# Hash attention and MoE on one core: projections of two groups of pairs in three parts, transposes spread out, values prepared per pair

## The chip, the core and the metric

The kernel runs on one core of one Trainium2 chip; the other cores are idle and the granted TensorE clock (1.0 is full speed) is 0.998 to 1.0 in every run told here. The metric is device time in microseconds; a time is the median of several executions. All runs below are in the fast state. A time is 1.7 to 1.9 us longer than the span of the same execution's profile.

## The reference

Four batches of eight heads, 768 tokens, head size 64. Queries and keys are hashed to six bits by the sign of a projection, and a query sees only keys of its own bucket. The result goes through an MoE layer with a SiLU.

```python
q_bits = (np.einsum('bhsd,dk->bhsk', q, proj) > 0)          # 6 bits, likewise k
mask = q_bucket[:, :, :, None] == k_bucket[:, :, None, :]
scores = np.where(mask, scale * q @ k.T, -1e9)
attn = softmax(scores) @ v                                   # x = attn, heads side by side
h = x @ w_in                                                 # 3072 x 512 @ 512 x 2048
out = (h * sigmoid(h)) @ w_out
```

## The kernel before

Heads are taken in 16 pairs. A pair's q and k are transposed to `qk32` (64 rows of each head over one another), projected to bits, and the bits are written as extra rows beside q and k, so that one matmul gives score plus mask. The main loop counts units: each does one piece of 512 score columns, one exp on ScalarE (ACT) and four attention-times-value matmuls; nine units make a head. `plan(w, f)` puts preparation work ahead of unit `w`. In the traces here the instructions of an engine stand in the program's order (DVE's copies of unit 12's transposes, which TensorE started at 16.27 us, come only at 19.47, behind pair 1's bits), so the unit also decides the place in every engine's queue. From pair 6 on, q and k are transposed in blocks on DVE instead. The parts that matter:

```python
def warm_up(n):                       # ahead of any data, to open TensorE's clock
    for _ in range(n):
        nc.tensor.matmul(wps, warm, warm[:, None, :].to_broadcast([P, 4, P]), ...)
warm_up(5)
...
def t_unit(p, i):                     # 4 of the 12 transposes of a pair
    tp = ps.tile([P, 512], F32, tag="m", name="tp_ps", bufs=3)   # PSUM: three banks "m"
    for j in range(4): nc.tensor.transpose(tp[...], src[...], ident)
    nc.vector.tensor_copy(out=qk32[p][:, 512 * i : 512 * (i + 1)], in_=tp)
...
def v_unit(p, heads=(0, 1)):          # GpSimd, per head: cast v, and sum it over 6 blocks
    for i in heads:
        nc.gpsimd.tensor_copy(out=vv[:, :, 0:D], in_=src)
        nc.gpsimd.tensor_tensor(out=sa, in0=src[:, 0:3], in1=src[:, 3:6], op=ALU.add)
        nc.gpsimd.tensor_tensor(out=sb, in0=sa[:, 0], in1=sa[:, 1], op=ALU.add)
        nc.gpsimd.tensor_tensor(out=vs[:, i, 0:D], in0=sb, in1=sa[:, 2], op=ALU.add)
...
def proj_unit(*pairs):                # two pairs: 32 output rows for each of 4 (pair, q or k)
    for c0, w in ((0, 512), (512, S - 512)):
        bp = ps.tile([P, 512], F32, tag="m", name="bp_ps", bufs=3)
        ...                           # four narrow matmuls
    for bp, c0, w in bps:
        nc.vector.tensor_scalar(out=bt[...], in0=bp[...], ..., op0=ALU.is_gt, op1=ALU.subtract)
...
def av(w):
    if w % NU == 0:                   # first matmul of a head: needs vs, the sums of its v
        nc.tensor.matmul(o_ps[h][:, 0:NJ, :], dmat, vs[:, None, :].to_broadcast(...), ...)
...
for i in range(2):
    plan(8, lambda i=i: cast_unit(1, i))
    plan(8, lambda i=i: v_unit(1, (i,)))
plan(10, lambda: proj_halves(1))
for i in range(2):
    plan(11 + i, lambda i=i: bits_halves(1, i))       # each 4 instructions on VectorE (DVE)
for i in range(6):                                    # pairs 2, 3: units 12, 15, ..., 27
    plan(12 + 3 * i, lambda i=i: t_unit(2 + i // 3, i % 3))
    ...                                               # casts with the third of each pair
plan(28, lambda: proj_unit(2, 3))
...                                                   # pairs 4, 5: units 33, 36, ..., 48; projection in 60
```

The softmax here doesn't subtract the row's maximum and nothing guards it: scores larger than these inputs give would overflow.

Of the kernel before, what the change touches and what calls it, by code (L numbers as in the profile page):

```python
# [9 lines left out]
F32 = mybir.dt.float32  # L10
# [3 lines left out]
ALU = mybir.AluOpType  # L14
# [3 lines left out]
def kernel(  # L18
# [104 lines left out]
    def warm_up(n):  # L123
        for _ in range(n):
            nc.tensor.matmul(wps, warm, warm[:, None, :].to_broadcast([P, 4, P]),
                             start=True, stop=True)

    warm_up(5)
    ident = cst.tile([P, P], F32, name="ident")
    make_identity(nc, ident)  # L130

# [17 lines left out]
    NSL = 4  # L149
    QKA = [cst.tile([P, 2 * S], F16, name=f"qka{i}") for i in range(NSL)]  # L150
    QKB = [cst.tile([P, 2 * S], F16, name=f"qkb{i}") for i in range(NSL)]
    NVS = 8
    VV = [cst.tile([P, NJ, E1], F16, name=f"vv{i}") for i in range(NVS)]
    VS = [cst.tile([P, 2, E1], F16, name=f"vs{i}") for i in range(NVS // 2)]
    for i in range(NVS):
        nc.vector.memset(VV[i][:, :, D:E1], 1.0)
        nc.vector.memset(VS[i // 2][:, i % 2, D:E1], float(NJ))
    for i in range(NSL):
        (nc.vector if i < 2 else nc.gpsimd).memset(QKB[i][0:64, :], 0.0)
    ident16 = cst.tile([P, P], F16, name="ident16")  # L160
# [17 lines left out]
    def t_unit(p, i):  # L178
        if i == 0:
            qk32[p] = t32.tile([P, 2 * S], F32, tag="qk32", name="qk32")  # L180
        tp = ps.tile([P, 512], F32, tag="m", name="tp_ps", bufs=3)
        for j in range(4):
            n, t = divmod(4 * i + j, NJ)
            src = qk_sb[p, "qk"[n]]
            nc.tensor.transpose(tp[:, j * P : (j + 1) * P],  # L185
                                src[:, t].rearrange("p h d -> p (h d)"), ident)
        nc.vector.tensor_copy(out=qk32[p][:, 512 * i : 512 * (i + 1)], in_=tp)
# [64 lines left out]
                                scalar1=CS, scalar2=1.0,  # L252
                                op0=ALU.mult, op1=ALU.mult)

    def v_unit(p, heads=(0, 1)):
        for i in heads:
            h = 2 * p + i
            vv, vs = VV[h % NVS], VS[p % (NVS // 2)]
            src = v_sb[p][:, i, :].rearrange("p (t d) -> p t d", d=D)
            nc.gpsimd.tensor_copy(out=vv[:, :, 0:D], in_=src)  # L260
            sa = nrm.tile([P, 3, D], F32, tag="vsa", name="vsa")
            nc.gpsimd.tensor_tensor(out=sa, in0=src[:, 0:3], in1=src[:, 3:6], op=ALU.add)  # L262
            sb = nrm.tile([P, D], F32, tag="vsb", name="vsb")
            nc.gpsimd.tensor_tensor(out=sb, in0=sa[:, 0], in1=sa[:, 1], op=ALU.add)
            nc.gpsimd.tensor_tensor(out=vs[:, i, 0:D], in0=sb, in1=sa[:, 2], op=ALU.add)

    bits = {}
    CB = 256

    def proj_unit(*pairs):  # L270



        bt = btp.tile([P, 3, CB + 2], F16, tag="bits", name="bits")
        bps = []
        for c0, w in ((0, 512), (512, S - 512)):
            bp = ps.tile([P, 512], F32, tag="m", name="bp_ps", bufs=3)
            for i, p in enumerate(pairs):
                for n in range(2):
                    c = 32 * (2 * i + n)  # L280
                    nc.tensor.matmul(bp[c : c + 32, 0:w], pw[:, 0:32],  # L281
                                     qk32[p][:, n * S + c0 : n * S + c0 + w],
                                     start=True, stop=True)
            bps.append((bp, c0, w))
        r = slice(0, 64 * len(pairs))
        for bp, c0, w in bps:
            nc.vector.tensor_scalar(out=bt[r, c0 // CB : (c0 + w) // CB, 0:CB],
                                    in0=bp[r, 0:w].rearrange("d (x c) -> d x c", c=CB),
                                    scalar1=sc[r, 0:1], scalar2=sc[r, 1:2],
                                    op0=ALU.is_gt, op1=ALU.subtract)  # L290
        bits[pairs] = bt

    def proj_halves(p):

# [84 lines left out]

    def av(w):  # L380
        h, pts = parts(w)
        vv, vs = VV[h % NVS], VS[h // 2 % (NVS // 2)][:, h % 2, :]
        if w % NU == 0:
            o_ps[h] = ps.tile([P, NJ + 1, E1], F32, tag="o", name="o_ps", bufs=2)



            if direct(h):
                nc.tensor.matmul(o_ps[h][:, 0:NJ, :], dmat,  # L389
                                 vs[:, None, :].to_broadcast([P, NJ, E1]),  # L390
                                 start=True, stop=True)
        if w % NU == 4 and not direct(h):
            nc.tensor.matmul(o_ps[h][:, NJ, :], dmat, vs,
                             start=False, stop=True, skip_group_check=True)
        u = ut.pop(w)
        for jt, c0, n, o0 in pts:
            for i in range(n // P):
                nc.tensor.matmul(o_ps[h][:, c0 // P + i, :],  # L398
                                 u[:, o0 + i * P : o0 + (i + 1) * P], vv[:, jt, :],
                                 start=(not direct(h) and w % NU == 0 and i == 0), stop=True,  # L400
                                 skip_group_check=True)
        if w % NU == NU - 1:
            o = o_ps.pop(h)
            p, par = divmod(h, 2)
            if par == 0:
                x_pr[p] = xpl.tile([P, NJ, P], F16, tag="xpr", name="x_pr", bufs=4)
            if not direct(h):

                osum = nrm.tile([P, NJ, E1], F32, tag="osum", name="osum")
                vsum = nrm.tile([P, 1, E1], F32, tag="vsum", name="vsum")  # L410
                nc.vector.tensor_copy(out=vsum, in_=o[:, NJ : NJ + 1, :])
                nc.vector.tensor_tensor(  # L412
                    out=osum, in0=o[:, 0:NJ, :], in1=vsum.to_broadcast([P, NJ, E1]),
                    op=ALU.add)
                o = osum
            rec = nrm.tile([P, NJ], F32, tag="rec", name="rec")
            nc.vector.reciprocal(out=rec, in_=o[:, 0:NJ, D])  # L417
            (nc.vector if direct(h) else nc.gpsimd).tensor_tensor(  # L418
                out=x_pr[p][:, :, par * D : (par + 1) * D], in0=o[:, 0:NJ, 0:D],
                in1=rec[:, :, None].to_broadcast([P, NJ, D]), op=ALU.mult)  # L420
# [124 lines left out]
    t_first(0, 1, nc.vector.tensor_copy)  # L545
    warm_up(2)
    bt = proj_first(0)
    v_unit(0, (0,))
    for e in range(2):
        for n in range(2):  # L550
            cast_first(0, n, e, nc.scalar)
# [10 lines left out]
    def second_head():  # L562
        bt = proj_first(1)
        for e in range(2):
            for n in range(2):
                cast_first(1, n, e, nc.gpsimd)
                bits_first(bt, 1, n, e, nc.vector.tensor_copy)
        v_unit(0, (1,))

    at = {}  # L570

    def plan(w, fn):
        at.setdefault(w, []).append(fn)
# [4 lines left out]
        plan(4 + 2 * i, lambda i=i: t_unit(1, i))  # L578
    for i in range(2):
        plan(8, lambda i=i: cast_unit(1, i))  # L580
        plan(8, lambda i=i: v_unit(1, (i,)))
    plan(10, lambda: proj_halves(1))
    for i in range(2):
        plan(11 + i, lambda i=i: bits_halves(1, i))
        plan(0, lambda p=2 + i: load_qk(p))
        plan(3 + i, lambda p=2 + i: load_v(p))

    for i in range(6):
        plan(12 + 3 * i, lambda i=i: t_unit(2 + i // 3, i % 3))
        if i % 3 == 2:  # L590
            for par in range(2):
                plan(12 + 3 * i, lambda p=2 + i // 3, par=par: cast_unit(p, par))
    plan(28, lambda: proj_unit(2, 3))
    for i in range(4):
        plan(29 + i, lambda i=i: bits_unit((2, 3), i // 2, i % 2))
    for i in range(2):
        for j in range(2):
            plan(18 + 9 * i + 2 * j, lambda p=2 + i, j=j: v_unit(p, (j,)))
        plan(21 + i, lambda p=4 + i: load_qk(p))
    for i in range(4):  # L600
        plan((24, 40, 68, 74)[i], lambda i=i: load_w_in(i))
        plan(80 + 4 * i, lambda i=i: load_w_out(i))

    for i in range(6):
        plan(QST - 3 + 3 * i, lambda i=i: t_unit(4 + i // 3, i % 3))
        if i % 3 == 2:
            for par in range(2):
                plan(QST - 3 + 3 * i, lambda p=4 + i // 3, par=par: cast_unit(p, par))
    for Q in range(2, NQUAD):
        w0 = (Q - 1) * QST  # L610
        for i in range(4 if Q > 2 else 0):
            w1 = w0 + (5, 9, 12, 15)[i]
            plan(w1, lambda Q=Q, i=i: block_unit(2 * Q + i // 2, i % 2))
            if i % 2:
                for par in range(2):
                    plan(w1, lambda p=2 * Q + i // 2, par=par: cast_unit(p, par))
        wp = w0 + {2: 24, 3: 21}.get(Q, 20)
        plan(wp, lambda Q=Q: proj_unit(2 * Q, 2 * Q + 1))
        for i in range(4):
            plan(wp + {2: i, 3: 2 * i}.get(Q, 0),  # L620
                 lambda Q=Q, i=i: bits_unit((2 * Q, 2 * Q + 1), i // 2, i % 2))
        for i in range(2):
            plan(w0 + 5 + i, lambda p=2 * Q + i: load_v(p))
            for j in range(2):
                plan(w0 + 18 + 9 * i + 2 * j, lambda p=2 * Q + i, j=j: v_unit(p, (j,)))
            if Q + 1 < NQUAD:
                plan(w0 + (28 if Q == 3 else 8) + i, lambda p=2 * Q + 2 + i: load_blocks(p))
    for p in range(NPAIR):
# [73 lines left out]
```

## Time and profile before

| | before |
|---|---|
| time | 303.56 us (three runs, 303.19 to 303.80) |
| span of the profiled execution | 301.3 us |
| busy: TensorE (PE), DVE, ACT, GpSimd (POOL) | 98%, 60%, 70%, 43% |
| first exp | 8.26 us |
| first transposes of pair 4 (unit 33) | 28.88 us |
| first block transpose on DVE (unit 77) | 52.35 us |
| fourth block transpose on DVE (pair 7's k) | 61.82 us |

The lower four rows are landmarks that I use for every run: their differences cut the span into stretches, and a change in a stretch names the place where time went. The busy shares average over stages with different limits; the prediction reads the stages from the strips and the chain.

### The profile page before, as it was taken

What the parts mean: (1) busy time and instruction counts of PE and PEld (TensorE: products, weight loads), DVE (VectorE), ACT (ScalarE), POOL (GpSimd) and SP (SyncE); (2) the same over time, 40 slices, a digit from 0 to 9 for tenths busy, and PEclk for the clock granted to TensorE, in tenths of its full rate; (3) what the DMA queues carried; (4) which work ended last, traced back from release to release, by engine and by line L of the source; (5) the groups of instructions that cost most, each with busy time, mean ns of one, the idle gap of its engine ahead of it and who ended that gap; (6) DMA issues with size and microseconds to landing.
All of it is one profiled execution on the core that took longest, in us unless ns stands there. A gap on an engine that the chain in (4) does not pass through costs nothing.

```text
span 301.3 us, 7181 instructions
## 1 busy us (share of the span) xinstructions
PE 296.6 (98%) x2710; PEld 175.1 (58%) x2710; DVE 180.1 (60%) x344; ACT 210.1 (70%) x392; POOL 128.3 (43%) x203
## 2 busy tenths in 40 slices
PE   8999999999999999999999999999999999999996
PEld 3676855545665665555565665555566654446653
DVE  5797938899588355854694434954443443664332
ACT  5987989989886777778876666978977722452200
POOL 7589999388418551935158401755111100000000
PEclk9999999999999999999999999999999999999999
DMA  7999997999988638834078135011022003001112
GB/s 202 243 237 199 181 153 115 199 212 173 150 187 145 107 102 211 126 84 133 3 139 133 49 74 189 2 42 31 2 61 63 20 21 93 35 2 70 37 68 71
DMA packets 103170, 32.87 MB, mean 109 GB/s; under 512 B 90656, under 2 KB 100192, under 8 KB 103136
## 3 DMA queue, kind: packets, MB, share of 16 engines
q1 hardware_dynamic: 98752, 28.22, 44.6%
q0 software_dynamic: 4224, 4.19, 9.0%
q8 instruction: 21, 0.34, 0.5%
q14 instruction: 13, 0.11, 0.1%
q10 hardware_dynamic: 160, 0.00, 0.0%
HBM read 27.27 MB, written 6.29 MB: 111 GB/s over the span
## 4 chain that ended last, share of the span: by engine, by line
PE 88%; DVE 7%; DMA 1%; ACT 1%; issue 1%; SPq 1%; DVEq 0%; ACTq 0%
PE o_ps L496 26%; PE h_ps L461 24%; PE s_ps L366 19%; PE o_ps L398 12%; DVE g L470 3%; PE bp_ps L281 3%; PE tp_ps L185 2%; DMA k_row<-in_k_dram 1%; PE o_ps L482 1%; DVE qk L246 1%; DVE qka L343 1%; ACT u L369 1%; DVE osum L412 1%; SPq L79 0%; PE o_ps L389 0%
## 5 line engine op out<-in xcount | busy, mean ns | idle before, releaser
L369 ACT ACTIVATE u<-s_ps 128x512 f16<-128x512 f32 x288 | 157.0, 606 | 38.7 <-PE s_ps L366 38.3
L470 DVE SCALAR_TENSOR_TENSOR g<-th,h_ps 128x512 f16<-128x512 f32 x96 | 65.5, 687 | 73.8 <-ACT th L468 73.8
L461 PE MATMUL h_ps<-xT,win 128*128 128x512 f16 (+1 forms) x512 | 98.4, 325 | 0.1
L398 PEld LDWEIGHTS <-u 128*128 128x128 f16 x1152 | 68.1, 98 | 42.2 <-ACT u L369 8.4
L496 PE MATMUL o_ps<-wout,g 128*128 128x512 f16 x368 | 91.6, 379 | 0.0
L398 PE MATMUL o_ps<-vv,u 128*128 128x65 f16 x1152 | 82.6, 194 | 0.5 <-ACT u L369 0.4
L468 ACT ACTIVATE th<-h_ps 128x512 f32<-128x512 f32 x96 | 57.9, 603 | 35.9 <-PE h_ps L461 33.2
L461 PEld LDWEIGHTS <-win 128*128 128x128 f16 x512 | 49.9, 98 | 30.5 <-issue 0.4
L418 POOL TENSOR_TENSOR x_pr<-osum,rec 128x384 f16<-128x384 f32 x23 | 19.0, 826 | 88.5 <-DVE rec L417 88.0
L496 PEld LDWEIGHTS <-g 128*128 128x128 f16 x368 | 35.8, 98 | 33.7
L366 PE MATMUL s_ps<-qka 71*128 71x512 f16 x192 | 52.7, 327 | 0.0
L366 PE MATMUL s_ps<-qkb 128*128 128x512 f16 x192 | 52.6, 326 | 0.0
L251 POOL TENSOR_SCALAR qka<-qk 64x1536 f16<-64x1536 f32 x15 | 22.0, 1466 | 11.5 <-DVE qk L246 5.7
L501 DVE TENSOR_SCALAR osb<-o_ps 128x512 f32<-128x512 f32 x23 | 15.9, 691 | 15.0 <-PE o_ps L496 15.0
L251 POOL TENSOR_SCALAR qkb<-qk 64x1536 f16<-64x1536 f32 x15 | 22.1, 1471 | 1.2
L262 POOL TENSOR_TENSOR vsa<-v_sb 128x192 f32<-128x192 f32 x32 | 18.9, 591 | 0.0
L260 POOL CAST vv<-v_sb 128x384 f16<-128x384 f32 x32 | 16.2, 507 | 1.0 <-DMA v_sb<-in_v_dram 0.6
L246 DVE STREAM_TRANSPOSE qk<-k_blk 128x768 f32<-128x768 f32 x10 | 15.8, 1582 | 0.3 <-issue 0.3
L246 DVE STREAM_TRANSPOSE qk<-q_blk 128x768 f32<-128x768 f32 x10 | 16.0, 1596 | 0.0
L366 PEld LDWEIGHTS <-qka 71*128 71x128 f16 x192 | 15.5, 97 | 0.4 <-ACT qka L238 0.3
L366 PEld LDWEIGHTS <-qkb 128*128 128x128 f16 x192 | 15.4, 97 | 0.0
L412 DVE TENSOR_TENSOR osum<-o_ps,vsum 128x390 f32<-128x390 f32 x23 | 13.0, 565 | 2.3
(70 smaller groups left out, 162.5 us busy)
## 6 DMA issues: line engine op xcount, KB each, us to landing
out_dram<-osb SPq DMA_DIRECT2D x23, 256.0 KB
v_sb<-in_v_dram SPq DMA_DIRECT2D x15, 384.0 KB
q_blk<-in_q_dram SPq DMA_DIRECT2D x40, 96.0 KB
k_blk<-in_k_dram SPq DMA_DIRECT2D x40, 96.0 KB
win<-in_moe_w_in_dram POOLq DMA_DIRECT2D x4, 512.0 KB, 7.7
wout<-in_moe_w_out_dram POOLq DMA_DIRECT2D x4, 512.0 KB, 6.2
q_sb<-in_q_dram SPq DMA_DIRECT2D x5, 384.0 KB
k_sb<-in_k_dram SPq DMA_DIRECT2D x5, 384.0 KB
```

Of the source, the lines that this page charges most:

```text
L246: nc.vector.transpose(out=dst, in_=qk_sb[p, "qk"[n]])
L251: nc.gpsimd.tensor_scalar(out=dst[rows, :], in0=qk32[p][rows, :], scalar1=CS, scalar2=1.0, op0=ALU.mult, op1=ALU.mult)
L260: nc.gpsimd.tensor_copy(out=vv[:, :, 0:D], in_=src)
L262: nc.gpsimd.tensor_tensor(out=sa, in0=src[:, 0:3], in1=src[:, 3:6], op=ALU.add)
L366: nc.tensor.matmul(sp[:, o0 : o0 + n], t[rows, S + jt * P : S + (jt + 1) * P], t[rows, c0 : c0 + n], start=True, stop=True)
L369: nc.scalar.activation(out=u, in_=sp, func=AF.Exp, scale=ESC)
L398: nc.tensor.matmul(o_ps[h][:, c0 // P + i, :], u[:, o0 + i * P : o0 + (i + 1) * P], vv[:, jt, :], start=(not direct(h) and w % NU == 0 and ...
L418: (nc.vector if direct(h) else nc.gpsimd).tensor_tensor(out=x_pr[p][:, :, par * D : (par + 1) * D], in0=o[:, 0:NJ, 0:D], in1=rec[:, :, Non ...
L461: nc.tensor.matmul(hp[:, j, :], w_in16[:, dt, ft * P : (ft + 1) * P], xT[4 * b + dt][:, c0 : c0 + n], start=(dt == 0), stop=(dt == NDT - 1))
L468: nc.scalar.activation(out=th, in_=hp, func=AF.Tanh, scale=0.5)
L470: after.append(lambda: nc.vector.scalar_tensor_tensor(out=g[ci][:, grp * f : (grp + 1) * f, :], in0=th, scalar=1.0, in1=hp, op0=ALU.add, o ...
L496: nc.tensor.matmul(o2[tt], g[ci][:, ft, ct * P : (ct + 1) * P], w_out16[:, ft, :], start=(ft == 0), stop=(ft == NFT - 1))
```

## The change

The intent is to take the two long pauses out of ACT's stream of exps: each projection of two pairs becomes three parts of 256 columns some units apart, and the transposes that feed them alternate between the two pairs. The value preparation is done for both heads of a pair by instructions twice as large. The warm-up of TensorE partly uses narrow matmuls of 32 and 64 rows.

```diff
-    warm_up(5)
+    warm_up(1)
+    warm_rows(32, 2)     # 8 matmuls of 32 rows x 256 columns, in four row groups and PSUM banks
+    warm_up(1)
+    warm_rows(64, 2)     # 4 of 64 rows
+    warm_up(1)
...
-    def v_unit(p, heads=(0, 1)):
-        for i in heads:
-            ...
+    def v_unit(p, heads=slice(0, 2)):     # the same four instructions, for both heads at once
...
-    def proj_unit(*pairs):
+    def proj_unit(*pairs, parts=((0, 2), (2, 3))):
...
         plan(8, lambda i=i: cast_unit(1, i))
-        plan(8, lambda i=i: v_unit(1, (i,)))
+    plan(8, lambda: v_unit(1))
...
-    for i in range(6):
-        plan(12 + 3 * i, lambda i=i: t_unit(2 + i // 3, i % 3))
-        ...
-    plan(28, lambda: proj_unit(2, 3))
+    def prepare(p, steps, parts):
+        for k, w in enumerate(steps):
+            i, j = divmod(k, 2)
+            plan(w, lambda q=p + j, i=i: t_unit(q, i))
+            ...                           # casts with the third of each pair
+        for x, w in enumerate(parts):
+            plan(w, lambda x=x: proj_unit(p, p + 1, parts=((x, x + 1),)))
+    prepare(2, (12, 14, 16, 18, 21, 23), (20, 25, 28))
...
-    for i in range(6):
-        plan(QST - 3 + 3 * i, lambda i=i: t_unit(4 + i // 3, i % 3))      # 33 ... 48
-        ...
+    prepare(4, (33, 36, 39, 42, 48, 51), (45, 54, 58))    # and no projection in unit 60
...
-            for j in range(2):
-                plan(w0 + 18 + 9 * i + 2 * j, lambda ...: v_unit(p, (j,)))
+            plan(w0 + 18 + 9 * i, lambda p=2 * Q + i: v_unit(p))
```

More of the change, by code (lines that the diff above doesn't have):

```diff
@@ L126, in warm_up, with warm_rows @@
                              start=True, stop=True)
-    warm_up(5)
+    def warm_rows(size, n):
+        banks = [ps.tile([P, 2, P], F32, tag="s", name="warm_s", bufs=3) for _ in range(3)]
+        banks.append(wps[:, 0:2, :])
+        for _ in range(n):
+            for r in range(P // size):
+                w = warm[size * r : size * (r + 1)]
+                nc.tensor.matmul(banks[r], w, w[:, None, :].to_broadcast([size, 2, P]),
+                                 start=True, stop=True)
+    warm_up(1)
[3 more added lines that the diff above has]
+    warm_up(1)
     ident = cst.tile([P, P], F32, name="ident")
@@ L151 @@
     QKB = [cst.tile([P, 2 * S], F16, name=f"qkb{i}") for i in range(NSL)]
-    NVS = 8
-    VV = [cst.tile([P, NJ, E1], F16, name=f"vv{i}") for i in range(NVS)]
-    VS = [cst.tile([P, 2, E1], F16, name=f"vs{i}") for i in range(NVS // 2)]
+    NVS = 4
+    VV = [cst.tile([P, 2, NJ, E1], F16, name=f"vv{i}") for i in range(NVS)]
+    VS = [cst.tile([P, 2, E1], F16, name=f"vs{i}") for i in range(NVS)]
     for i in range(NVS):
-        nc.vector.memset(VV[i][:, :, D:E1], 1.0)
-        nc.vector.memset(VS[i // 2][:, i % 2, D:E1], float(NJ))
+        nc.vector.memset(VV[i][:, :, :, D:E1], 1.0)
+        nc.vector.memset(VS[i][:, :, D:E1], float(NJ))
     for i in range(NSL):
@@ L253, in cast_unit @@
                                 op0=ALU.mult, op1=ALU.mult)
-    def v_unit(p, heads=(0, 1)):
-        for i in heads:
-            h = 2 * p + i
-            vv, vs = VV[h % NVS], VS[p % (NVS // 2)]
-            src = v_sb[p][:, i, :].rearrange("p (t d) -> p t d", d=D)
-            nc.gpsimd.tensor_copy(out=vv[:, :, 0:D], in_=src)
-            sa = nrm.tile([P, 3, D], F32, tag="vsa", name="vsa")
-            nc.gpsimd.tensor_tensor(out=sa, in0=src[:, 0:3], in1=src[:, 3:6], op=ALU.add)
-            sb = nrm.tile([P, D], F32, tag="vsb", name="vsb")
-            nc.gpsimd.tensor_tensor(out=sb, in0=sa[:, 0], in1=sa[:, 1], op=ALU.add)
-            nc.gpsimd.tensor_tensor(out=vs[:, i, 0:D], in0=sb, in1=sa[:, 2], op=ALU.add)
+    def v_unit(p, heads=slice(0, 2)):
+        n = heads.stop - heads.start
+        vv, vs = VV[p % NVS][:, heads], VS[p % NVS][:, heads]
+        src = v_sb[p][:, heads].rearrange("p h (t d) -> p h t d", d=D)
+        nc.gpsimd.tensor_copy(out=vv[:, :, :, 0:D], in_=src)
+        sa = nrm.tile([P, n, 3, D], F32, tag="vsa", name="vsa")
+        nc.gpsimd.tensor_tensor(out=sa, in0=src[:, :, 0:3], in1=src[:, :, 3:6], op=ALU.add)
+        sb = nrm.tile([P, n, D], F32, tag="vsb", name="vsb")
+        nc.gpsimd.tensor_tensor(out=sb, in0=sa[:, :, 0], in1=sa[:, :, 1], op=ALU.add)
+        nc.gpsimd.tensor_tensor(out=vs[:, :, 0:D], in0=sb, in1=sa[:, :, 2], op=ALU.add)
     bits = {}
     CB = 256
-    def proj_unit(*pairs):
-        bt = btp.tile([P, 3, CB + 2], F16, tag="bits", name="bits")
+    def proj_unit(*pairs, parts=((0, 2), (2, 3))):
+        if pairs not in bits:
+            bits[pairs] = btp.tile([P, 3, CB + 2], F16, tag="bits", name="bits")
+        bt = bits[pairs]
         bps = []
-        for c0, w in ((0, 512), (512, S - 512)):
+        for x0, x1 in parts:
+            c0, w = x0 * CB, (x1 - x0) * CB
             bp = ps.tile([P, 512], F32, tag="m", name="bp_ps", bufs=3)
@@ L283, in proj_unit @@
                                      start=True, stop=True)
-            bps.append((bp, c0, w))
+            bps.append((bp, x0, x1))
         r = slice(0, 64 * len(pairs))
-        for bp, c0, w in bps:
-            nc.vector.tensor_scalar(out=bt[r, c0 // CB : (c0 + w) // CB, 0:CB],
-                                    in0=bp[r, 0:w].rearrange("d (x c) -> d x c", c=CB),
+        for bp, x0, x1 in bps:
+            nc.vector.tensor_scalar(out=bt[r, x0:x1, 0:CB],
+                                    in0=bp[r, 0 : (x1 - x0) * CB]
+                                    .rearrange("d (x c) -> d x c", c=CB),
                                     scalar1=sc[r, 0:1], scalar2=sc[r, 1:2],
                                     op0=ALU.is_gt, op1=ALU.subtract)
-        bits[pairs] = bt
     def proj_halves(p):
@@ L381, in av @@
         h, pts = parts(w)
-        vv, vs = VV[h % NVS], VS[h // 2 % (NVS // 2)][:, h % 2, :]
+        vv, vs = VV[h // 2 % NVS][:, h % 2], VS[h // 2 % NVS][:, h % 2, :]
         if w % NU == 0:
@@ L547 @@
     bt = proj_first(0)
-    v_unit(0, (0,))
+    v_unit(0, slice(0, 1))
     for e in range(2):
@@ L567, in second_head @@
                 bits_first(bt, 1, n, e, nc.vector.tensor_copy)
-        v_unit(0, (1,))
+        v_unit(0, slice(1, 2))
     at = {}
@@ L586 @@
         plan(3 + i, lambda p=2 + i: load_v(p))
-    for i in range(6):
-        plan(12 + 3 * i, lambda i=i: t_unit(2 + i // 3, i % 3))
-        if i % 3 == 2:
-            for par in range(2):
-                plan(12 + 3 * i, lambda p=2 + i // 3, par=par: cast_unit(p, par))
-    plan(28, lambda: proj_unit(2, 3))
+    def prepare(p, steps, parts):
+        for k, w in enumerate(steps):
+            i, j = divmod(k, 2)
+            plan(w, lambda q=p + j, i=i: t_unit(q, i))
+            if i == 2:
+                for par in range(2):
+                    plan(w, lambda q=p + j, par=par: cast_unit(q, par))
+        for x, w in enumerate(parts):
+            plan(w, lambda x=x: proj_unit(p, p + 1, parts=((x, x + 1),)))
+    prepare(2, (12, 14, 16, 18, 21, 23), (20, 25, 28))
     for i in range(4):
@@ L596 @@
     for i in range(2):
-        for j in range(2):
-            plan(18 + 9 * i + 2 * j, lambda p=2 + i, j=j: v_unit(p, (j,)))
+        plan(18 + 9 * i, lambda p=2 + i: v_unit(p))
         plan(21 + i, lambda p=4 + i: load_qk(p))
@@ L602 @@
         plan(80 + 4 * i, lambda i=i: load_w_out(i))
-    for i in range(6):
-        plan(QST - 3 + 3 * i, lambda i=i: t_unit(4 + i // 3, i % 3))
-        if i % 3 == 2:
-            for par in range(2):
-                plan(QST - 3 + 3 * i, lambda p=4 + i // 3, par=par: cast_unit(p, par))
+    prepare(4, (33, 36, 39, 42, 48, 51), (45, 54, 58))
     for Q in range(2, NQUAD):
@@ L617 @@
         wp = w0 + {2: 24, 3: 21}.get(Q, 20)
-        plan(wp, lambda Q=Q: proj_unit(2 * Q, 2 * Q + 1))
+        if Q > 2:
+            plan(wp, lambda Q=Q: proj_unit(2 * Q, 2 * Q + 1))
         for i in range(4):
@@ L623 @@
             plan(w0 + 5 + i, lambda p=2 * Q + i: load_v(p))
-            for j in range(2):
-                plan(w0 + 18 + 9 * i + 2 * j, lambda p=2 * Q + i, j=j: v_unit(p, (j,)))
+            plan(w0 + 18 + 9 * i, lambda p=2 * Q + i: v_unit(p))
             if Q + 1 < NQUAD:
```

## The prediction

> **What bounds the kernel now.** I read the page first.
>
> ```profile
> PE 296.6 (98%) x2710; PEld 175.1 (58%) x2710; DVE 180.1 (60%) x344; ACT 210.1 (70%) x392; POOL 128.3 (43%) x203
> DVE  5797938899588355854694434954443443664332
> ACT  5987989989886777778876666978977722452200
> ```
>
> TensorE looks full everywhere, but a matmul's modelled span hides waits behind it, so the 98% alone names no bound. The strips show stages: ACT is nearly full in slices 3 to 8 (15 to 60 us), DVE in slice 9 (60 to 68 us), neither later. The chain that ended last agrees: from 76 us on it is TensorE matmuls with 0.2 us steps of other engines between them, from 55 to 76 us it runs over DVE (g, block transposes, bits), before that over TensorE and ACT. The change edits the program before unit 72 (about 51 us) and the GpSimd work of all pairs. What it gains or loses must arise before 51 us and is then handed on by the later stages, whose work is unchanged.
>
> A unit is one score, one exp and one attention-times-value step. Third view: the timeline of ACT from 16 to 48 us. Columns: start, length, instruction, count, idle time just before.
>
> ```profile
> 16.19 9.54 ACT L369 ACTIVATE u<-s_ps 128x512 f16<-128x512 f32 x18 [0.64 <-PE s_ps L366]
> 27.39 16.27 ACT L369 ACTIVATE u<-s_ps 128x512 f16<-128x512 f32 x32 [1.65 <-PE s_ps L366]
> 44.76 3.54 ACT L369 ACTIVATE u<-s_ps 128x512 f16<-128x512 f32 x7 [1.11 <-PE s_ps L366]
> ```
>
> Two idle stretches, 1.65 and 1.11 us, each for a late score. Fourth view: the chain in order of time at the same two places (start, length, what).
>
> ```profile
> 24.83 0.22 PE s_ps L366
> 25.04 1.80 PE bp_ps L281 x15
> 26.84 0.23 PE o_ps L398 x4
> 27.07 0.23 PE s_ps L366 x2
> ...
> 42.58 0.22 PE s_ps L366
> 42.80 1.43 PE bp_ps L281 x16
> 44.22 0.23 PE o_ps L398 x4
> 44.45 0.21 PE s_ps L366
> ```
>
> So the projections of pairs 2,3 (unit 28) and 4,5 (unit 60) hold TensorE while ACT runs dry. 1.65+1.11 = 2.76 us is the most that spreading them can give. Fifth view: the timeline of DVE while pairs 2 and 3 are transposed.
>
> ```profile
> 16.52 1.46 DVE L320 COPY qka<-bits 13x384 f16<-13x384 f16 x4
> 18.01 0.34 DVE L320 COPY qkb<-bits 13x384 f16<-13x384 f16 x1
> 18.37 0.40 DVE L317 TENSOR_SCALAR qkb<-bits,sc 13x384 f16<-13x384 f16 x1
> 18.78 0.34 DVE L320 COPY qkb<-bits 13x384 f16<-13x384 f16 x1
> 19.14 0.41 DVE L317 TENSOR_SCALAR qkb<-bits,sc 13x384 f16<-13x384 f16 x1
> 19.47 1.27 DVE L187 COPY qk<-tp_ps 128x512 f32<-128x512 f32 x2
> 20.67 0.17 DVE L417 RECIPROCAL rec<-o_ps 128x6 f32<-128x6 f32 x1
> 20.87 0.56 DVE L418 TENSOR_TENSOR x_pr<-o_ps,rec 128x384 f16<-128x384 f32 x1
> 21.35 1.28 DVE L187 COPY qk<-tp_ps 128x512 f32<-128x512 f32 x2
> ```
>
> DVE is late here. TensorE did the first transposes (unit 12) at 16.27, DVE copied them out only at 19.47, after the bits of pair 1. This backlog decides my number.
>
> **What the Trainium skill says.** "TensorEngine Tiling (Array Packing)", Key Properties: changing the tiling mode drains TensorE. The trace agrees in size: score to score over the projection at 42.58 takes 1.87 us, a bare unit 0.34 (17.33 to 17.67), so the projection costs 1.53. At full clock its columns need 12 waves of 256 column times; at the 0.43 us that one 512-column wave pair shows between its weight loads (42.73, 43.18, 43.61) that is 1.28. The remaining 0.25 is entering and leaving the narrow mode. "TensorE: Matmul & The Clock Gate", Part 3, The mechanism: a weight load overlaps running matmuls only in other row groups; no row-tiled matmul is in this trace. The same page, Part 1, has a cold and a warm clock, about a factor of two; the trace agrees: the first five warm-up matmuls start 0.42 us apart, the two at 4.54 take 0.59 together. "Perfetto Trace Analysis", Optimizing Scalar/DVE Operations: instructions have a fixed cost, so larger ones help only a saturated engine; GpSimd shows such a cost below.
>
> **The change part by part.**
> *Three parts instead of one.* Same columns, but three entries into the narrow mode. A part is 0.43+0.25 = 0.68 us, three are 2.04 against 1.53: +0.5 us of TensorE work for each of the two projections, now in pieces. The bits comparison on DVE becomes three of 0.53 instead of 0.81+0.53, +0.26 us, and its first parts move earlier.
>
> *Pairs 2 and 3.* TensorE from unit 12 (16.27) to the value step of unit 28 (26.77) takes 10.5 us. After the change it must do 16 units at 0.34, six transposes at 0.44, three parts at 0.68 and two first-matmuls at 0.17: 5.44+2.64+2.04+0.34 = 10.46. So TensorE itself, not the bunching, sets this stretch, and there is nothing to gain even without new waits. (The old projection cost 1.90 here, 24.83 to 27.07 less 0.34, because it waited for the copy of the transposes one unit earlier. That is saved and pays for the extra drains.)
>
> New waits come on top. Transposes are now in units 12, 14, 16, 18; they share three PSUM banks. The one of unit 18 needs the bank of unit 12, which DVE frees at 19.47+0.6 = 20.1; TensorE reaches it at 16.27+6x0.34+3x0.44 = 19.6: a wait of 0.5. The first part in unit 20 needs that transpose copied. DVE in order: copies of units 12, 14, 16 from 19.47 (0.6 each) to 21.3, the reciprocal and product of head 1 (0.7) to 22.0, then unit 18's copy to 22.6. TensorE is there at about 21.4, so it waits 1.1 or so. From 22.65: the part without its entry 0.5, eight units 2.72, two transposes 0.88, 0.17, two parts 1.36: 28.3 against 26.77. That is +1.5 us.
>
> *Pairs 4 and 5.* I count TensorE's lag behind ACT: a unit of ACT is 0.49 (from the stretch 38 to 42 us), of TensorE 0.34, so 0.15 is recovered per unit, and a lag over about 0.45 starves ACT (that figure reproduces the 1.11). Before: little until unit 60, then 0.04+1.53-0.15 = 1.42, about 1.0 lost, and 0.14 in unit 45. After: the parts fall in units 45 and 54, each with the first matmul of a head (0.17), and 58, with the six transposes of pair 2's result (0.34). Each peaks near 0.13+0.85-0.15 = 0.83, or 0.87 in unit 58, and loses about 0.4: 1.2 against 1.25. Change: 0, give or take 0.3.
>
> *Start.* Five cold matmuls of 0.42 become three, plus eight narrow ones of 32 rows and four of 64. If all of a group ran together the time would be the same 2.1 us; with weight loads of 0.13 to 0.15 between them and drains, I take 0.3 to 1 us more. The first score, at 8.01, waits for the second head: its k lands at 6.77, three transposes 0.55, three warm matmuls 0.65. The first head has some 0.3 us to spare. So +0.1 us, rather than the full delay.
>
> *Values per pair.* GpSimd's adds take 0.320 us at 64 elements and 0.591 at 192: 0.0021 per element and 0.185 fixed. Twice 0.51+0.59+0.32+0.32 = 3.48 becomes about 0.84+1.0+0.455+0.455 = 2.75 per pair, so 11 us of GpSimd over 15 pairs, none of it on the chain: no step of it has GpSimd.
>
> Sum of the working: +1.5+0+0.1 = +1.6, so 305.2 us.
>
> **Rivals.**
> 1. The spread works as meant: ACT never runs dry in units 20 to 60, up to 2.76 us gained, about 301. For it: both gaps are real, and steps this irregular look tuned. Against it: 10.46 against 10.5 us of TensorE work.
> 2. My wait on the DVE backlog (1.5 us), the working above. For it: the copies stand in DVE's queue in this order, and the changed program has waits on DVE ahead of the transposes of unit 18 and of the first part. Against it: none of these waits exists in the trace of before.
> 3. Without rival 2's waits, but with the extra drains, all cancels: 303.5.
> 4. The narrow warm-ups run one by one at the cold clock and delay the first head by 2 us: +0.5 to 1 more, near 306.
> 5. Narrow warm-ups open the clock earlier: no gain, as the first score waits for k.
>
> **Range and chances.** I believe the working at about 60%, but a tuned change is rarely slower, so I take some of the 1.6 back: 304.6 us. The range 302.0 to 306.0 holds rivals 2, 3 and half of 1. Two per cent is 6 us, more than twice the largest gap, so within 2% has 0.97; 0.02 for faster, 0.01 for slower.
>
> **What would show each step right or wrong.** In the changed trace: the wait of TensorE for DVE before the transposes of unit 18 and the first part, in all about 1.6 us near 20 to 23 us, with an ACT gap over 1 us there; the last value step before unit 29 near 28.3 instead of 26.77; no gap of 1.11 near 44 but three of about 0.4; chain of 76 us on shifted unchanged; GpSimd near 117 us busy. I am wrong if ACT has no gap over 0.5 between 16 and 48 us (then rival 1), or if the first score starts more than 0.5 us from 8.0 (then the warm-ups matter), or if the time between unit 72 and the end changes by over 0.5 us.

## The result, and the profile after

The changed kernel takes 305.56 us (six runs, 305.21 to 307.53) against 303.39 us of the kernel before (six runs): 2.17 us more by the medians. The ratio is 1.0087, with a 95% interval of 1.0061 to 1.0114. Ratios here and below are the mean time of one kernel's fast runs over that of the other's in the same rounds, so they are not quite the ratio of the medians. The change is under 2%, and slower.

First the page of the kernel after: busy times, then the strips of DVE and ACT.

```profile
PE 298.7 (98%) x2736; PEld 175.6 (57%) x2736; DVE 181.1 (59%) x338; ACT 210.7 (69%) x392; POOL 118.2 (39%) x143
DVE  4796949789859444854596335854543342664332
ACT  4877999987987686878876666878878732452200
```

GpSimd lost 10.1 us of work as meant, TensorE gained 2.1 us, and the strips have the same stages. Nothing here says where the time went. The timeline of ACT does (start, length, instruction, count, idle time before).

```profile
22.50 1.09 ACT L381 ACTIVATE u<-s_ps 128x512 f16<-128x512 f32 x2 [0.95 <-PE s_ps L378]
24.74 0.60 ACT L381 ACTIVATE u<-s_ps 128x512 f16<-128x512 f32 x1 [1.16 <-PE s_ps L378]
28.46 10.32 ACT L381 ACTIVATE u<-s_ps 128x512 f16<-128x512 f32 x20 [0.73 <-PE s_ps L378]
39.16 4.59 ACT L381 ACTIVATE u<-s_ps 128x512 f16<-128x512 f32 x9 [0.39 <-PE s_ps L378]
44.06 2.07 ACT L381 ACTIVATE u<-s_ps 128x512 f16<-128x512 f32 x4 [0.30 <-PE s_ps L378]
46.67 9.61 ACT L381 ACTIVATE u<-s_ps 128x512 f16<-128x512 f32 x19 [0.55 <-PE s_ps L378]
```

The one gap of 1.65 us became 0.95, 1.16 and 0.73; the one of 1.11 became 0.39, 0.30 and 0.55. TensorE's timeline at the first two gaps (transpose of unit 18, first part in unit 20):

```profile
21.09 0.44 PE L198 MATMUL tp_ps<-ident,q_sb 128*128 128x128 f32 x2 [0.39 <-DVE qk L200]
23.58 0.62 PE L293 MATMUL bp_ps<-qk,pw 128*32 128x256 f32 x2 [0.27 <-DVE qk L200]
```

The idle figures here are short because the modelled spans of earlier matmuls reach into them. The weight loads of the same two groups show the whole waits, 0.69 and 0.75 us:

```profile
21.09 0.20 PEld L198 LDWEIGHTS tp_ps<-ident,q_sb 128*128 128x128 f32 x2 [0.69 <-DVE qk L200]
23.58 0.14 PEld L293 LDWEIGHTS bp_ps<-qk,pw 128*32 128x32 f32 x2 [0.75 <-DVE qk L200]
```

And DVE in that time:

```profile
20.03 0.41 DVE L329 TENSOR_SCALAR qkb<-bits,sc 13x384 f16<-13x384 f16 x1
20.37 1.86 DVE L200 COPY qk<-tp_ps 128x512 f32<-128x512 f32 x3
22.16 0.17 DVE L429 RECIPROCAL rec<-o_ps 128x6 f32<-128x6 f32 x1
22.37 0.56 DVE L430 TENSOR_TENSOR x_pr<-o_ps,rec 128x384 f16<-128x384 f32 x1
22.84 0.68 DVE L200 COPY qk<-tp_ps 128x512 f32<-128x512 f32 x1
```

DVE starts its copies only after pair 1's bits. The transposes at 21.09 wait for the first of the three, the part at 23.58 for the copy at 22.84. The profiled execution was the slowest of the six (307.53 us) and shows one more wait, on DVE, in the stretch after unit 77:

```profile
65.96 1.55 DVE L259 STREAM_TRANSPOSE qk<-k_blk 128x768 f32<-128x768 f32 x1 [1.34 <-DMA k_blk<-in_k_dram]
```

The load of pair 7's k was late in that execution. In the twelve further traces below, which have the same instructions there, this stretch is at most 0.6 us longer than before, so I put it down to this execution and not to the median. (A second of the six, 306.77 us, is also over 1 us above the median; it has no trace.) By landmarks, all in us; "rest" runs to the last record of the trace, at 301.34 and 305.76 us:

| kernel | first exp | first exp to pair 4 | pair 4 to unit 77 | unit 77 to 4th block transpose | rest |
|---|---|---|---|---|---|
| before | 8.26 | 20.62 | 23.47 | 9.47 | 239.52 |
| after | 9.17 | 22.33 | 23.55 | 10.91 | 239.80 |

Without the start and the late load, the change is +1.71 +0.08 +0.28 = 2.07 us, close to the 2.17 of the medians. The experiments check each of these terms, and the two that I left out.

### The profile page after: what moved, and what is told of

The parts are those of the page before. It is cut to its first block, busy times and chain, and to the rows that moved or that the text cites. A ratio compares the mean times of both kernels' runs of the same rounds, so it can differ in the third digit from the quotient of the medians.

```text
span 305.8 us, 7166 instructions
## 1 busy us (share of the span) xinstructions
PE 298.7 (98%) x2736; PEld 175.6 (57%) x2736; DVE 181.1 (59%) x338; ACT 210.7 (69%) x392; POOL 118.2 (39%) x143
## 4 chain that ended last, share of the span: by engine, by line
PE 86%; DVE 7%; DMA 4%; ACT 1%; issue 1%; SPq 0%; POOL 0%; ACTq 0%; DVEq 0%; POOLq 0%
PE o_ps L508 26%; PE h_ps L473 23%; PE s_ps L378 17%; PE o_ps L410 10%; DMA k_blk<-in_k_dram 4%; PE bp_ps L293 3%; PE tp_ps L198 2%; DVE g L482 2%; PE o_ps L494 1%; ACT u L381 1%; PE warm_ps L125 1%; DVE qk L200 1%; DVE qka L355 1%; PE bp_ps L238 1%; DVE qk L259 1%
## 5 line engine op out<-in xcount | busy, mean ns | idle before, releaser
L274 POOL TENSOR_TENSOR vsa<-v_sb 128x384 f32<-128x384 f32 (+1 forms) x17 | 16.1, 949 | 0.0
L272 POOL CAST vv<-v_sb 128x768 f16<-128x768 f32 (+1 forms) x17 | 13.4, 788 | 1.1 <-DMA v_sb<-in_v_dram 0.8
```

The costliest lines, as they stand in the source:

```text
L274: nc.gpsimd.tensor_tensor(out=sa, in0=src[:, :, 0:3], in1=src[:, :, 3:6], op=ALU.add)
```

## The experiments

My theory after reading the result: TensorE's waits on DVE's backlog make the 1.7 us, pairs 4,5 gain nothing, and the rest of the change is beside the chain. The rivals: the extra entries into the narrow mode; the start; the values. Twelve kernels were run, all gave correct results, all were fast, all with five rounds. First each part of the change alone, on the kernel before (with the values' tiles laid out as after, which only drops eight memsets at the start).

**only_warm: the narrow warm-ups alone.**

```diff
-    warm_up(5)
+    warm_up(1); warm_rows(32, 2); warm_up(1); warm_rows(64, 2); warm_up(1)
```

> The kernel before with the narrow warm-ups alone. In the profile of the changed kernel the first exp starts at 9.17 us instead of 8.26. Theory A (the narrow warm-ups delay the first head, mostly because TensorE's clock opens later): +0.6 to +1.0 us, first exp near 9.2, and the two wide warm-ups after the first transposes take about 1.0 us together instead of 0.59. Theory B (the later start was chance of that one profile; the prediction's +0.1): below +0.3 us.

Measured: 303.56 against 303.41 us, ratio 0.9997 (0.9978 to 1.0015). Theory A falls. The two wide warm-ups after the first transposes did take 1.06 us and the first exp started at 8.73, but they also took 1.06 us, with a first exp at 9.17, in only_q2 below, which has the five wide ones. Over all 14 profiles the first exp lies between 8.26 and 9.19, with either warm-up. The clock record in the trace files, whose start no view of `prof` shows, tells what moves it: its first entry, at full clock, lies between 4.29 and 7.20 us in the 13 traces that have one, and the earlier it is, the earlier, on the whole, the first exp (4.39 and 8.26 in the kernel before, 7.20 and 9.19 in best, both with five wide warm-ups; 4.29 and 8.28 in after_bits_late, 6.54 and 9.17 in the changed kernel, both with narrow ones). With the same warm-up the opening differs by over 2 us between executions, so these few traces show no effect of the kind of warm-up; the landmark "first exp" must be taken out before two profiles are compared.

**only_q1: pairs 2,3 alone.**

```diff
-    ... t_unit in units 12, 15, 18, 21, 24, 27;  plan(28, lambda: proj_unit(2, 3))
+    prepare(2, (12, 14, 16, 18, 21, 23), (20, 25, 28))
```

> The kernel before with only pairs 2,3 in three parts and their transposes in units 12,14,16,18,21,23. Theory A (TensorE waits for DVE's backlog before the transposes of unit 18 and the first part): +1.4 to +1.8 us, waits on DVE of 0.7 and 0.8 us in the trace, ACT gaps of about 1 us twice near 20 to 24 us. Theory B (in the changed kernel the waits only took the place of the late start): below +0.5.

Measured: 305.87 against 303.41 us, ratio 1.0073 (1.0053 to 1.0094). First exp to pair 4: 22.33 us, exactly the changed kernel's; the later stretches up to the fourth block transpose are as before. Theory A holds: this part alone makes the 1.71 us. The profiled execution lost another 1.2 us in its rest, at 111 us, to a score that waited for the DMA of bits:

```profile
111.13 0.38 PE L374 MATMUL s_ps<-qka 71*128 71x512 f16 x1 [1.03 <-DMA qka<-bits]
```

No other trace has that, and the instructions there are those of before, so I count it as chance. (Three of the six executions lie at 306.2 us or above, so it may not be rare; that was not followed up.) One wait here I had not named: the transposes of unit 14 waited 0.9 us for pair 3's q to land. The total did not rise by it: in this trace it stands in place of DVE's wait before the transposes of unit 18, and 0.65 us for DVE remain before the first part. So only one of theory A's two waits is seen here; both are in the changed kernel's trace.

**only_q2: pairs 4,5 alone.**

```diff
-    ... t_unit in units 33, 36, ..., 48;  projection in unit 60
+    prepare(4, (33, 36, 39, 42, 48, 51), (45, 54, 58))
```

> The kernel before with only pairs 4,5 in three parts and their transposes in units 33 to 51. Theory A (the gap of 1.11 us is broken in three of 0.3 to 0.55 whose sum is about the same, extra drains eat the rest): 0 to +0.4 us. Theory B (spreading pays once the pairs 2,3 are not late): -0.5 to -1.0 us.

Measured: 303.99 against 303.41 us, ratio 1.001 (0.9992 to 1.0028). Pair 4 to unit 77: 23.80 against 23.47 us, +0.33; the ACT gaps are 0.65, 0.30 and 0.55 instead of 1.11. Theory A: spreading gains nothing here.

**only_v: the values per pair alone.**

```diff
-        plan(8, lambda i=i: v_unit(1, slice(i, i + 1)))     # cast, values, cast, values
+    plan(8, lambda: v_unit(1))                              # cast, cast, values of both heads
     (and likewise, one call per pair, for pairs 2 to 15)
```

> The kernel before with only the value preparation once per pair. Theory A (GpSimd is off the chain): within 0.2 us of before with GpSimd near 118 us busy. Theory B (moved casts and weight loads change the DMA order and the block loads of pair 7 come late): +0.5 us or more, with a wait of DVE for the DMA of k in blocks.

Measured: 304.91 against 303.41 us, ratio 1.0047 (1.0024 to 1.0069). Both theories miss. First exp to pair 4 is 21.71 us, +1.09, and the trace shows why. Before, GpSimd (times in us; line, instruction):

```profile
16.83 0.59 POOL L262 TENSOR_TENSOR vsa<-v_sb 128x192 f32<-128x192 f32 x1
17.90 0.32 POOL L265 TENSOR_TENSOR vs<-vsb,vsa 128x64 f16<-128x64 f32 x1
```

and in only_v, with TensorE's first matmul of pair 1's first head:

```profile
19.11 1.00 POOL L270 TENSOR_TENSOR vsa<-v_sb 128x384 f32<-128x384 f32 x1
20.72 0.46 POOL L273 TENSOR_TENSOR vs<-vsb,vsa 128x128 f16<-128x128 f32 x1
21.23 0.33 PE L397 MATMUL o_ps<-vs,dmat 128*128 128x390 f16 x1 [0.93 <-POOL vs L273]
```

Unit 18 needs only head 0's sums. Before, they were done at 18.2 us, between the two casts; now they come with head 1's, after both casts, at 21.2. The work is less and the result is later. The other 0.4 us of this run lie behind the last DVE instruction, see after_both.

Now parts of the change undone, on the changed kernel.

**after_v_early: pair 1's values ahead of the casts.**

```diff
-    plan(8, lambda: v_unit(1))
+    plan(6, lambda: v_unit(1))
```

> The changed kernel with pair 1's value preparation moved from unit 8 to unit 6, ahead of the two casts. Alone, the merged value preparation cost 1.09 us between the first exp and the transposes of pair 4 (21.71 against 20.62). Theory A (in the changed kernel that wait lies inside the waits on DVE): the stretch stays at 22.2 to 22.4 us, time 305.2 to 305.7. Theory B (the two waits add up): the stretch falls by about 1 us, time about 304.5.

Measured: 305.91 against 303.47 us, ratio 1.0086 (1.0063 to 1.0108); the stretch is 22.34 us. Theory A: in the changed kernel the wait for the values lies inside the waits for DVE. Costs measured one by one (1.71 and 1.09) don't add up when the same stretch holds both.

**after_bits_late: pair 1's second bits out of DVE's way.**

```diff
-        plan(11 + i, lambda i=i: bits_halves(1, i))
+        plan((11, 19)[i], lambda i=i: bits_halves(1, i))
```

> The changed kernel with the second half of pair 1's bits (four DVE instructions, 1.5 us) moved from unit 12 to unit 19, so that DVE copies the transposes out earlier. Theory A (DVE's backlog makes the wait): the waits of TensorE on DVE before unit 18's transpose and the first part vanish, but the wait for pair 1's values at unit 18, hidden until now, comes out: the stretch from the first exp to pair 4's transposes 21.5 to 21.9 us instead of 22.33, time about 305.0. Theory B (three entries into the narrow mode make the loss): no change, 22.3.

Measured: 304.87 against 303.47 us, ratio 1.0042 (1.003 to 1.0054); the stretch is 21.77 us. The waits on DVE are gone and 0.56 us with them, so the backlog is the cause and theory B falls. But what came out instead was not the values; it was the load that only_q1 had shown:

```profile
18.28 0.66 PE L198 MATMUL tp_ps<-ident,q_sb 128*128 128x128 f32 x4 [0.71 <-DMA q_sb<-in_q_dram]
```

Its weight load waited 0.99 us. This execution had an early first exp (8.28), and pair 3's q, now wanted seven units sooner, was not there. The values were then in time (20.79, first matmul at 21.01).

**after_both: both moves.**

```diff
-    plan(8, lambda: v_unit(1))
+    plan(6, lambda: v_unit(1))
-        plan(11 + i, lambda i=i: bits_halves(1, i))
+        plan((11, 19)[i], lambda i=i: bits_halves(1, i))
```

> The changed kernel with both moves. Theory A: neither wait is left, the stretch is 20.5 to 20.9 us as before the change (20.62), time 303.4 to 304.0, since TensorE's work there is the same within 0.1 us. Theory B (spreading pays once the waits are gone): below 20.0 us, time below 303.0. Theory C (drains): above 21.2.

Measured: 304.51 against 303.47 us, ratio 1.0033 (1.0021 to 1.0045); the stretch is 20.92 us, at the edge of what theory A expected, and the trace has no wait of TensorE on DVE, GpSimd or a load there that the kernel before lacks. With the two waits of 0.69 and 0.75 us added it gives 22.36, and the changed kernel has 22.33. Theories B and C fall: without waits, three parts take 0.30 us more than the one piece did before, which itself waited for a copy. The time lies 0.5 us over the expected range. One part of that is the end, which I had forgotten: after the last DVE instruction the profile of before runs 2.51 us on, this one 2.77, only_v and after 2.92 and 2.80. (All stretches behind the first exp add up to +0.62 us, the medians to +1.04; the other 0.4 is not found in this trace, which is of the fastest execution.) What SyncE waited for at the end (total, times, longest), first in the kernel before, then in the changed one:

```profile
SPq L697 <- PEq L697: 0.7, 2, 0.5
```

```profile
SPq L710 <- PEq L710: 1.0, 2, 0.8
```

All seven kernels with values per pair have 0.2 to 0.4 us more in the rest than the kernel before; those with values per head do not (only_q1's 1.2 aside). SyncE's wait names TensorE's sequencer, but the records of the closing instructions, which `prof`'s timeline leaves out, put the delay in GpSimd's own: between its DRAIN and its clearing of the semaphores lie 0.03 us in the seven kernels with values per head and 0.32 to 0.34 in six of the seven with values per pair; in only_v the DRAIN itself starts late and takes 0.24 us instead of 0.10. The other engines' last instructions come after that. So the end is a pause in GpSimd's instruction stream. What makes the pause was not tested and stays open.

**only_v_early: the values per pair alone, pair 1's in unit 6.**

```diff
-    plan(8, lambda: v_unit(1))
+    plan(6, lambda: v_unit(1))
```

> The kernel before with the value preparation once per pair, and pair 1's in unit 6 instead of 8. Theory A (alone, the merge cost 1.09 us only because pair 1's sums came late for the first matmul of unit 18): no wait for GpSimd there, first exp to pair 4's transposes 20.6 us, time within 0.3 us of before. Theory B (larger GpSimd instructions cost something later too): still +0.4 us or more.

Measured: 304.16 against 303.53 us, ratio 1.0016 (0.9996 to 1.0037). First exp to pair 4 is 20.64 us: the wait is gone, as theory A has it. Of the +0.42 in the rest, 0.29 is the end again, and this execution also had 0.5 us of waiting for a load of k in blocks before it.

**both_one_proj: both moves, and the projection of pairs 2,3 in one piece.**

```diff
-    prepare(2, (12, 14, 16, 18, 21, 23), (20, 25, 28))
+    prepare(2, (12, 14, 16, 18, 21, 23), ())
+    plan(28, lambda: proj_unit(2, 3))
```

> The changed kernel with both moves (pair 1's values in unit 6, its second bits in unit 19) and the projection of pairs 2,3 in one piece in unit 28, the transposes spread as changed. Theory A (two more entries into the narrow mode cost 0.25 us each): first exp to pair 4's transposes 20.92-0.51 = 20.4 us, time 0.5 us under that of the three parts. Theory B (parts pay once the waits are gone): over 21.0.

Measured: 304.62 against 303.53 us, ratio 1.003 (1.001 to 1.005). The stretch is 20.30 us, 0.62 under the three parts, against 0.51 expected from two saved entries. But the time is not lower: the next stretch is 0.31 longer (23.86 against 23.55), where weight loads of pairs 4,5's parts wait for DVE, whose copies of the transposes come late:

```profile
PEld bp_ps L293 <- DVE qk L200: 0.8, 3, 0.3
```

Two of these three waits, of 0.24 us each, stand in after_both too, one of them put down to issue; the new one is 0.27 us inside the first part (35.53), which so takes 0.98 us to the next weight load instead of 0.65. Half of the gain was given back; the other half is within the noise of the times (this kernel's six lie between 303.76 and 305.36).

**best: a version meant to beat both.**

```diff
     (kernel before, and)
-        plan(12 + 3 * i, lambda i=i: t_unit(2 + i // 3, i % 3))
+        plan((12, 15, 18, 21, 23, 25)[i], lambda i=i: t_unit(2 + i // 3, i % 3))
-    projection of pairs 4,5 in unit 60, bits in units 60 to 63
+    three parts in units 52, 56, 62, bits in units 63 to 66
```

> A version meant to beat both: the kernel before, with the last two transposes of pair 3 in units 23 and 25 (so that the single projection in unit 28 doesn't wait for their copy), and only pairs 4,5 in three parts, in units 52, 56 and 62, where TensorE is idle most, their bits from unit 63. By the lag count the first saves about 0.38 us, the second 0.6 to 0.7: time 302.2 to 302.6. If only unit 60's gap is moved about: 303.2 or more.

Measured: 303.57 against 303.47 us, ratio 0.9996 (0.9984 to 1.0008). The first idea worked (20.15 against 20.62 us). The second did not: pair 4 to unit 77 rose to 23.79, since the later bits stand ahead of pair 3's result in DVE's queue and the transposes of that result in unit 75 waited for it, 0.8 us at their weight load.

**best_q1: the first idea alone.**

> The kernel before with only the last two transposes of pair 3 in units 23 and 25. Same stretch as in the run before (20.15 against 20.62 us), all later stretches as before: 0.4 to 0.5 us under before, 303.0. If the gain is given back later: 303.4.

Its edit is the first half of the diff above. Measured: 302.96 against 303.53 us, ratio 0.9977 (0.9962 to 0.9993). The stretch is 20.16 us and all later ones as before. One projection that does not wait for its last transposes gains 0.46 us; no part of the change is needed for it.

**best_two: with pairs 4,5 in parts, but the bits in their old place.**

```diff
-    three parts in units 52, 56, 62, bits in units 63 to 66
+    three parts in units 52, 56, 60, bits in units 60 to 63
```

> That, and pairs 4,5 in three parts in units 52, 56 and 60 with the bits where they were, so that pair 3's result isn't late for its transposes in unit 75: pair 4's transposes to the first block transpose 23.1 to 23.3 us instead of 23.47, time 302.6 to 302.9. If DVE's bits are late again: no better than 303.0.

Measured: 302.86 against 303.53 us, ratio 0.9976 (0.9962 to 0.999): faster than before by 0.24%, and than the changed kernel by 2.7 us of medians, though those are from different rounds. ACT's timeline:

```profile
25.20 1.57 ACT L377 ACTIVATE u<-s_ps 128x512 f16<-128x512 f32 x3 [0.34 <-PE s_ps L374]
27.61 12.35 ACT L377 ACTIVATE u<-s_ps 128x512 f16<-128x512 f32 x24 [0.83 <-PE s_ps L374]
44.84 5.50 ACT L377 ACTIVATE u<-s_ps 128x512 f16<-128x512 f32 x11 [0.27 <-PE s_ps L374]
```

The gap of 1.65 us is 0.34 and 0.83, that of 1.11 is three of 0.22 to 0.27. Pair 4 to unit 77 takes 23.14 us. Against best_q1 the time is the same within the intervals; only the stretches (0.34 less) say that the parts in the right units help. The landmarks of all runs:

| kernel | first exp | first exp to pair 4 | pair 4 to unit 77 | unit 77 to 4th block transpose | rest |
|---|---|---|---|---|---|
| only_warm | 8.73 | 20.63 | 23.47 | 9.49 | 239.51 |
| only_q1 | 8.53 | 22.33 | 23.48 | 9.46 | 240.71 |
| only_q2 | 9.17 | 20.63 | 23.80 | 9.50 | 239.50 |
| only_v | 8.67 | 21.71 | 23.46 | 9.49 | 239.91 |
| after_v_early | 8.77 | 22.34 | 23.56 | 9.45 | 239.80 |
| after_bits_late | 8.28 | 21.77 | 23.56 | 9.49 | 239.76 |
| after_both | 8.75 | 20.92 | 23.55 | 9.46 | 239.77 |
| only_v_early | 8.97 | 20.64 | 23.47 | 10.06 | 239.94 |
| both_one_proj | 8.59 | 20.30 | 23.86 | 9.49 | 239.75 |
| best | 9.19 | 20.15 | 23.79 | 9.47 | 239.53 |
| best_q1 | 8.47 | 20.16 | 23.48 | 9.48 | 239.50 |
| best_two | 8.94 | 20.16 | 23.14 | 9.49 | 239.46 |

## Why the prediction was right or wrong

The main mechanism was right and the forecast was too small: about 1 us of loss was stated (304.6 against 303.56), 2.17 us were measured. The measured time lies in the stated range.

- **"I take some of the 1.6 back"** is the step that failed first. The working gave 305.2, and the runs gave 305.56; I moved away from it because a tuned change is rarely slower. No line of the profile stood behind that. The traces bear the working out instead: the two named waits exist and sit where it put them, and undoing their cause (after_bits_late) removes them. Their sizes were off one by one, 0.69 us instead of 0.5 and 0.75 instead of 1.1, and near in sum, 1.44 instead of 1.6.
- **Pairs 2 and 3, +1.5 us.** Measured 1.71, in only_q1 and in the changed kernel alike. With the first exp's 0.91 us of later start taken off, the value step of unit 20 follows its part at 23.22 (predicted about 23.2) and that of unit 28 starts at 28.49 (predicted 28.3). "Nothing to gain even without new waits" is borne out by after_both, 20.92 against 20.62: the 1.71 us are 1.44 of waits and about 0.3 of the split itself.
- **Pairs 4 and 5, 0 give or take 0.3.** Measured +0.33 alone and +0.08 within the changed kernel. The three gaps were 0.39, 0.30 and 0.55 against 0.4 each. The lag count was good enough to place the parts better in best_two, and it missed what DVE's queue did to best.
- **Start, +0.1 us.** Measured nothing (ratio 0.9997), and the delay of 0.3 to 1 us that it starts from was 0.21 (the first transposes start at 3.57 us instead of 3.36): the weight loads expected between the narrow warm-ups overlapped them, and eight took 0.55 us. The first exp 0.91 us later, which by my own sign would have stood against me, follows the clock's opening. My other sign, over 0.5 us between unit 72 and the end, is also met in the profile alone, by the late load.
- **"none of it on the chain: no step of it has GpSimd"** was wrong as a reason. That an engine is not on the chain of before says nothing of what happens when its results come later. Alone, the merge put 1.09 us there; in the changed kernel this was hidden behind the waits for DVE (after_v_early), so that it cost the sum nothing in that stretch was luck. What it did cost is about 0.28 us at the end of the span, a term that the working does not have.
- The sum so becomes 1.71 + 0.08 + 0 + 0.28 = 2.07 instead of 1.6. Of the rivals, number 1 fell (gaps of 0.95, 1.16 and 0.73 remain), number 2 held, number 3 is what after_both shows, bar the end, and number 4 fell with only_warm. Number 5 foresaw no gain and there was none; whether the narrow warm-ups open the clock earlier can't be told from so few traces.
- Not settled: what makes GpSimd pause at the end, and whether the values would be late in the changed kernel once DVE is not; in after_bits_late the load came first.

## What to carry to other kernels

Before splitting work to fill gaps, add up the busiest engine's work between the gaps: here TensorE had 10.46 us to do in a stretch of 10.5 once the projection was split, and there was nothing to fill; what there was to gain, 0.46 us, lay in one piece that does not wait (best_q1). Moving a producer earlier moves its consumers into another engine's queue; write down that queue in order, with its buffers, and see who stands ahead. Merging instructions saves their fixed cost but delivers the first result with the last, so look for the reader that needed only the first half.

## What the Trainium skill lacked or had wrong

- "TensorEngine Tiling (Array Packing)", Key Properties, says that a change of mode drains TensorE, but gives no cost. Here one projection of 1.53 us had, by the prediction's estimate, 0.25 us of entering and leaving the 32-column mode, and taking two entries out shortened the stretch by 0.62 us (20.92 to 20.30), somewhat more than 0.51.
- "TensorE: Matmul & The Clock Gate", Part 3, The mechanism, says that weight loads overlap running matmuls only when their row groups differ. Other row groups do overlap: in the changed kernel eight warm-ups of 32 rows and 256 columns took 0.55 us (in the chain, from 1.61 to the next wide one at 2.16), with the clock still closed, two groups of four side by side, although each has its own weight load. The "only" does not hold here: at 287.3 us in the kernel before, full-array matmuls of 512 columns start 0.216 us apart, and the 0.098 us weight load of the next begins as the one before it begins.
- The same page, Part 1, calls the moment of the clock's opening run-variable, by 0.5 us either way under sustained matmuls, and its cost small. The runs agree that it varies, but by more: the clock record starts between 4.29 and 7.20 us in 13 traces (with short pauses of TensorE before it). The first exp lies between 8.26 and 9.19 us over 14 profiles, which is more than most effects studied here. The page does not say that profiles must be lined up behind it.
- I found no page on a cost at a program's end that depends on one engine's program: GpSimd's pause before it clears the semaphores was 0.03 us before and 0.33 after, with its instructions down from 203 to 143.
